# A drain behind each GpSimd mask, clamp and cast in an attention and ELU feed-forward kernel

## The chip, the core and the metric

The kernel runs on one core of a Trainium2 chip. The metric is device time in microseconds: how long one execution takes on the chip. A core has five engines that run their own instruction streams side by side and wait for each other through semaphores: TensorE (PE, matmuls), VectorE (DVE), ScalarE (ACT), GpSimd (POOL) and SyncE (SP, which issues most transfers here). Transfers run on 16 DMA engines that all issuers share.

## What is computed

Attention with a causal mask over 576 positions, in front of which stand 16 "beacon" keys and values that every position may see; then a feed-forward layer with an ELU on the attention's output. 8 batches, 8 heads of 64, model width 512, inner width 2048.

```python
k_all = np.concatenate([beacon_k, k], axis=2)          # 16 + 576 keys
v_all = np.concatenate([beacon_v, v], axis=2)
scores = scale * np.matmul(q, k_all.transpose(0, 1, 3, 2))
causal[:, Nb:] = np.triu(np.ones((S, S), dtype=bool), k=1)
scores = np.where(causal, -1000000000.0, scores)
a = np.exp(scores - scores.max(-1, keepdims=True))
a /= a.sum(-1, keepdims=True) + 1e-09
out = np.matmul(a, v_all)                              # then (B * S, H * D)
h = x @ w_in
g = np.where(h > 0.0, h, np.exp(np.minimum(h, 0.0)) - 1.0)
return g @ w_out
```

## The kernel before

All work is written down first as a list of small operations (`Op`, lines 118 to 122), each with its engine or a choice of engines, the operations that it depends on, and the buffers that it takes and gives back. `Program.run` (lines 133 to 165) then goes through the table `ORDER`, made by hand, and emits the operations one by one. `PICKS` settles the engine where there is a choice (the letters P, V, A, G, S stand for TensorE, VectorE, ScalarE, GpSimd and SyncE), and `PLACES` settles the buffer. Nothing is moved afterwards: each engine runs its instructions in this order. The semaphores between engines are put in by the framework.

**Attention**, per batch and pair of heads. Loads of q, k and v go out on SP's queue (in the first batch on ACT's too) into float32 staging buffers (`st`, `vst`). A cast to 16 bits follows (`copy`, called from line 349 for a cast or a copy on DVE or POOL and from line 347 on ACT), into `sb` for q and k and into `v16` for v. For batches 0 to 3 PE transposes q and k (lines 393 to 453) and DVE and ACT copy them out of PSUM; from batch 4 on DMA transposes do it (line 508). Scores are matmuls with keys along the partitions (L542); the exponential is ACT's (L552), into a buffer `et`. The mask is POOL's (L557): an affine select that sets to zero what lies behind the diagonal, in place, in `et`. Then PE multiplies probabilities and values (L571), with a column of ones in v that gives the row sums, and DVE divides (L584, L585). The result is transposed by PE (L600) in batches 0 and 1 and by DMA (L591) from batch 2 on, into `xT`, a ring of three batches.

**Feed-forward**, in tiles of tokens: 128, 128 and 256 at first, then 512 each. A step is one bank of 512 columns: PE multiplies `xT` and `w_in` (L623), ACT takes the exponential (L630), the clamp brings that to at most 1 and at least 0, in place, in a buffer `wide` (L638 on POOL or DVE, in another form on ACT at L636), and DVE joins it with the matmul's own result, which gives ELU (L649). The second matmul with `w_out` is plain in the three small tiles (L760); the tiles of 512 tokens use a scheme of seven products in place of eight (L705), for which DVE forms sums and differences (L678 to L687, L722). Results go out from `wide`.

**Weights.** `w_in` and `w_out` come in four parts each, eight loads in all, which POOL issues (`load_w`, line 528, issue at L533). They are float32 in memory and are made float16 on the way. In POOL's order they stand between masks, clamps and casts of the first batches and small tiles: four parts of `w_in` first, then four of `w_out`.

POOL thus has five kinds of work: 142 masks, 72 clamps, 59 casts, 8 weight loads, and a few fills at the start. A mask is waited for by PE (L571), a clamp by DVE (L649), a cast of q and k by PE (L442 and others) or by SP (L508), and a cast of v by PE. SP also waits for casts, since a staging buffer can be loaded again only after its cast. In the first 25 us PE also runs 80 matmuls on a tile of ones, written into banks that nobody uses at that time (L352, the negative entries in `ORDER`).

The functions that the change touches, and what calls them:

Of the kernel before, what the change touches and what calls it, by code (L numbers as in the profile page):

```python
# [124 lines left out]
class Program:  # L125
# [7 lines left out]
    def run(self, order, picks, places, fill):  # L133

        picks, places, used = iter(picks), iter(places), set()
        for op in self.ops:  # L140
            if len(op.engines) > 1:
                op.eng = next(picks)
                assert op.eng in op.engines
        for i in order:
            if i < 0:
                at = int(next(places), 36)
                assert ("bank", at) not in used
                fill(self.rooms["bank"][at])
                continue
            op = self.ops[i]  # L150
            assert not op.done and all(d.done for d in op.deps)
            got = []
            for room in op.take:
                at = int(next(places), 36)
                assert (room, at) not in used
                used.add((room, at))
                op.held.append((room, at))
                got.append(self.rooms[room][at])
            if op.fn is not None:
                op.fn(self.engines[op.eng], *got, *op.args)  # L160
            for other, i in op.give:
                used.remove(other.held[i])
            op.done = True
        kept = {room for op in self.ops if op.keep for room in op.held}
        assert all(op.done for op in self.ops) and used == kept and next(places, None) is None
# [927 lines left out]
```

## Time and profile before

| | us |
|---|---|
| three runs | 335.48, 337.19, 337.56 (median 337.19) |
| the profiled execution | 334.36 |
| its span, from the first to the last instruction | 332.6 |
| PE busy | 324.6 |
| ACT, DVE, POOL busy | 244.4, 254.0, 160.2 |
| POOL: masks (L557), clamps (L638), casts into `sb` from `st` (L349) | 63.4, 45.1, 29.5 |
| longest sum of waits on POOL: clamps for ACT (L630), masks for ACT (L552) | 62.5, 54.1 |

How to read the lines in the next part: a row of the timeline has the start and the length in us, the engine, the line of the kernel, the operation, the tiles written and read, the shape, a count, and in brackets how long the engine had been idle before and what ended that. A row with a count above 1 stands for instructions that follow each other. In a table of stages the columns are the stretch, its length, the busy time with the number of instructions, the clock that TensorE was granted, the mean share of the DMA engines at work and the GB/s moved. A row of a source line has the count of the instructions, then their durations in ns (least, median, most) and the first and last start. An engine's name with a q behind it is its sequencer, which issues transfers and runs drains and semaphore instructions; those are not counted as busy.

### The profile page before, as it was taken

What the parts mean: (1) busy time and instruction counts of PE and PEld (TensorE: products, weight loads), DVE (VectorE), ACT (ScalarE), POOL (GpSimd) and SP (SyncE); (2) the same over time, 40 slices, a digit from 0 to 9 for tenths busy, and PEclk for the clock granted to TensorE, in tenths of its full rate; (3) what the DMA queues carried; (4) which work ended last, traced back from release to release, by engine and by line L of the source; (5) the groups of instructions that cost most, each with busy time, mean ns of one, the idle gap of its engine ahead of it and who ended that gap; (6) DMA issues with size and microseconds to landing.
All of it is one profiled execution on the core that took longest, in us unless ns stands there. A gap on an engine that the chain in (4) does not pass through costs nothing.

```text
span 332.6 us, 9782 instructions
## 1 busy us (share of the span) xinstructions
PE 324.6 (98%) x3784; PEld 233.9 (70%) x3784; DVE 254.0 (76%) x587; ACT 244.4 (73%) x475; POOL 160.2 (48%) x289
## 2 busy tenths in 40 slices
PE   8999999999999999999999999999999999999995
PEld 6678877545678558878847787557877895456884
DVE  4687786689997499667869984699639973889862
ACT  2797799887986985789989957887678835766410
POOL 3596995376767472474544531645165500214100
PEclk9999999999999999999999999999999999999999
DMA  7999999899866878595599956996480065000015
GB/s 214 248 246 229 218 271 239 246 314 200 159 181 113 163 173 197 114 169 109 106 190 205 159 120 184 197 155 134 110 153 34 33 143 169 0 3 32 21 55 179
DMA packets 131902, 51.43 MB, mean 155 GB/s; under 512 B 113424, under 2 KB 128272, under 8 KB 131856
## 3 DMA queue, kind: packets, MB, share of 16 engines
q1 hardware_dynamic: 122160, 41.47, 59.8%
q0 software_dynamic: 4224, 4.19, 7.6%
q10 hardware_dynamic: 5472, 5.15, 5.3%
q8 instruction: 29, 0.48, 0.6%
q14 instruction: 17, 0.14, 0.1%
HBM read 37.22 MB, written 9.44 MB: 140 GB/s over the span
## 4 chain that ended last, share of the span: by engine, by line
PE 84%; DMA 5%; POOL 3%; DVE 3%; issue 2%; ACT 1%; SPq 0%; POOLq 0%; DVEq 0%
PE bank L623 36%; PE bank L705 28%; PE bank L571 8%; PE bank L542 6%; PE bank L760 4%; DMA w_in<-in_moe_w_in_dram 3%; POOL et L557 2%; PE bank L442 1%; DMA st<-in_k_dram 1%; DMA st<-in_q_dram 1%; DVE gt L684 1%; DVE gt L649 1%; POOL sb L349 1%; DVE ss L678 0%; POOL w_in L533 0%
## 5 line engine op out<-in xcount | busy, mean ns | idle before, releaser
L623 PE MATMUL bank<-xT,w_in 128*128 128x512 f16 (+5 forms) x832 | 132.9, 314 | 0.4 <-DMA w_in<-in_moe_w_in_dram 0.3
L552 ACT ACTIVATE et<-bank 128x512 f16<-128x512 f32 (+3 forms) x220 | 108.5, 588 | 20.8 <-PE bank L542 18.0
L649 DVE SCALAR_TENSOR_TENSOR gt<-wide,bank 128x512 f16<-128x512 f32 x144 | 94.2, 688 | 23.1 <-POOL wide L638 14.1
L623 PEld LDWEIGHTS <-w_in 128*128 128x128 f16 x832 | 71.0, 98 | 48.7 <-issue 1.1
L630 ACT ACTIVATE wide<-bank 128x512 f32<-128x512 f32 x144 | 83.0, 600 | 25.1 <-PE bank L623 22.5
L557 POOL TENSOR_SCALAR_AFFINE_SELECT et<-et 128x256 f16<-128x256 f16 (+3 forms) x142 | 63.4, 467 | 55.2 <-ACT et L552 54.1
L705 PEld LDWEIGHTS <-gt 128*128 128x128 f16 x768 | 72.6, 98 | 13.8 <-issue 1.7
L638 POOL TENSOR_SCALAR wide<-wide 128x512 f32<-128x512 f32 x72 | 45.1, 633 | 70.8 <-ACT wide L630 62.5
L705 PE MATMUL bank<-w_out,gt 128*128 128x256 f16 x512 | 63.2, 273 | 0.0
L349 POOL CAST sb<-st 128x1024 bf16<-128x1024 f32 (+6 forms) x32 | 29.5, 931 | 21.9 <-DMA st<-in_q_dram 13.0
L571 PE MATMUL bank<-v,et 128*128 128x65 f16 (+1 forms) x960 | 37.9, 193 | 0.5 <-issue 0.5
L571 PEld LDWEIGHTS <-et 128*128 128x128 f16 (+1 forms) x960 | 35.4, 97 | 4.1 <-issue 1.2
L585 DVE TENSOR_TENSOR x<-bank,rl 128x256 f16<-128x256 f32 (+2 forms) x68 | 32.1, 472 | 2.4
L347 ACT ACTIVATE wide<-bank 128x512 f32<-128x512 f32 x24 | 14.4, 608 | 25.9 <-PE bank L705 23.8
L542 PE MATMUL bank<-qT,kT 64*128 64x80 bf16 (+4 forms) x752 | 32.9, 224 | 0.1
L705 PE MATMUL bank<-wt,gt 128*128 128x256 f16 x256 | 31.6, 273 | 0.9 <-DVE gt L684 0.5
L542 PEld LDWEIGHTS <-kT 64*128 64x128 bf16 x752 | 20.8, 95 | 12.0 <-issue 8.8
L638 DVE TENSOR_SCALAR wide<-wide 128x512 f32<-128x512 f32 x34 | 16.2, 477 | 10.8 <-ACT wide L630 10.7
L636 ACT ACTIVATE wide<-wide 128x512 f32<-128x512 f32 x38 | 23.9, 631 | 0.8
L722 DVE TENSOR_TENSOR wide<-bank,wide 128x512 f32<-128x512 f32 x24 | 16.3, 686 | 9.1 <-PE bank L705 6.4
L349 DVE COPY kT<-bank 128x16 bf16<-128x16 bf16 (+4 forms) x48 | 16.2, 448 | 6.4 <-PE bank L450 2.5
L584 DVE RECIPROCAL rl<-bank 128x4 f32<-128x4 f32 (+2 forms) x68 | 12.3, 181 | 10.8 <-PE bank L571 8.0
(64 smaller groups left out, 249.2 us busy)
## 6 DMA issues: line engine op xcount, KB each, us to landing
vst<-in_v_dram SPq DMA_DIRECT2D x23, 256.0 KB, 4.5
out_dram<-wide SPq DMA_DIRECT2D x18, 256.0 KB, 2.6
out_dram<-wide ACTq DMA_DIRECT2D x17, 256.0 KB, 2.7
st<-in_q_dram SPq DMA_DIRECT2D x16, 256.0 KB, 4.8
st<-in_k_dram SPq DMA_DIRECT2D x12, 256.0 KB, 4.2
w_in<-in_moe_w_in_dram POOLq DMA_DIRECT2D x4, 512.0 KB, 9.9
w_out<-in_moe_w_out_dram POOLq DMA_DIRECT2D x4, 512.0 KB, 9.9
st<-in_k_dram SPq DMA_DIRECT2D x7, 288.0 KB, 6.7
```

The costliest lines, as they stand in the source:

```text
L349: e.tensor_copy(out=out, in_=in_)
L542: e.matmul(out=banks[h][:, o:o + w], lhsT=kT[D * h:D * h + D, P * jc:P * jc + P], rhs=qT[D * h:D * h + D, q0:q0 + w], start=True, stop=Tru ...
L552: e.activation(out=et[:, h, 0:w], in_=scs[n, u][h][:, 0:w], func=AFT.Exp, bias=0.0, scale=float(1.0 / (D ** 0.5)))
L557: e.affine_select(out=part, in_=part, compare_op=ALU.is_ge, fill=fill0, base=q0 + NB - P * jc, pattern=[[0, 2], [0, times], [1, dw]], chan ...
L571: e.matmul(out=av[:, c:c + D + 1], lhsT=ets[tuple(unit)][0:m, h, col:col + P], rhs=v16s[b % 2][0:m, jc, 2 * hp + h, 0:D + 1], start=(jc == ...
L585: e.tensor_tensor(out=x16s[b % 2][:, blks[0]:blks[-1] + 1:step, P * hp:P * hp + P].rearrange("q i (h d) -> q i h d", d=D), in0=av[:, :, :, ...
L623: e.matmul(out=bank[:, o:o + z - a], lhsT=w_in16[:, cc, P * fc:P * fc + P], rhs=xTa[:, cc, a % RING:a % RING + z - a], start=(cc == 0), st ...
L630: e.activation(out=t, in_=hpss[p, i], func=AFT.Exp, bias=0.0, scale=1.0)
L636: e.activation(out=t, in_=t, func=AFT.Relu, bias=1.0, scale=-1.0)
L638: e.tensor_scalar(out=t, in0=t, scalar1=1.0, scalar2=0.0, op0=ALU.min, op1=ALU.max)
L649: e.scalar_tensor_tensor(out=out, in0=in0, scalar=-1.0 if (p, i) in below else 1.0, in1=in1, op0=ALU.mult if (p, i) in below else ALU.subt ...
L705: e.matmul(out=bank[:, HC * s:HC * s + HC], lhsT=left[:, c, P * s:P * s + P], rhs=RIGHT[k][:, fc], start=(fc == 0 and s == 0 and k in HEAD ...
```

## The change

Behind each operation that `Program.run` emits on GpSimd, except for the weight loads, a drain is emitted on GpSimd. A drain is an instruction without operands: the engine goes on to its next instruction when what it has under way is finished.

```diff
             if op.fn is not None:
                 op.fn(self.engines[op.eng], *got, *op.args)
+                if op.eng == "G" and op.fn.__name__ != "load_w":
+                    self.engines["G"].drain()
             for other, i in op.give:
                 used.remove(other.held[i])
             op.done = True
```

In the built program these are 273 drains on POOL, one behind each mask, clamp and cast. None of them waits for a semaphore or raises one. All other instructions stand on their engines in the order that they had, with the same buffers. The masks, clamps and casts raise the semaphores that they raised before. Only which of eight semaphores some of the transfers on SP's and ACT's queues raise is shifted, and with it the names in the waits for those transfers. The line numbers behind line 160 are two higher in the changed kernel: L557 becomes L559, and so on.

## Prediction

> **What bounds the kernel now.** I read the page of the profile first: busy shares, then the chain that ended last.
>
> ```profile
> PE 324.6 (98%) x3784; PEld 233.9 (70%) x3784; DVE 254.0 (76%) x587; ACT 244.4 (73%) x475; POOL 160.2 (48%) x289
> ...
> PE 84%; DMA 5%; POOL 3%; DVE 3%; issue 2%; ACT 1%; SPq 0%; POOLq 0%; DVEq 0%
> ```
>
> PE is busy 98% of the 332.6 us span and carries 84% of the chain. POOL is at work for 48%, so the average says that it has time to spare. But PE has none: what POOL delivers late, after PE's instruction in line has been reached, is lost for good, since PE's order is fixed. So the question is where POOL has no idle time. The table of POOL's busy time by stage answers it; its columns are the stretch, its length, then busy time and instructions.
>
> ```profile
> 13.30:17.66 4.36, 4.35 (x10) 1.00 1.08 263
> 17.66:49.79 32.13, 28.57 (x51) 1.00 1.15 239
> 49.79:56.98 7.19, 4.93 (x11) 1.00 1.17 241
> ```
>
> ```profile
> 60.00:80.00 20.00, 12.65 (x20) 1.00 1.10 279
> 80.00:100.00 20.00, 12.94 (x21) 1.00 0.79 173
> 100.00:120.00 20.00, 12.54 (x24) 1.00 0.77 153
> 120.00:150.00 30.00, 16.18 (x31) 1.00 0.79 155
> ```
>
> From 13.30 to 49.79 POOL is nearly full (32.9 of 36.5 us); behind 60 it works some 63% of the time or less. The head is therefore the place. POOL's timeline there (start, length, line, count, and in brackets the idle time ahead):
>
> ```profile
> 13.31 0.42 POOL L557 TENSOR_SCALAR_AFFINE_SELECT et<-et 128x256 f16<-128x256 f16 x1 [2.42 <-ACT et L552]
> ...
> 14.35 1.53 POOL L557 TENSOR_SCALAR_AFFINE_SELECT et<-et 128x256 f16<-128x256 f16 x4
> ...
> 17.67 0.90 POOL L533 DMA_DIRECT2D w_in<-in_moe_w_in_dram  x1
> 18.59 0.63 POOL L557 TENSOR_SCALAR_AFFINE_SELECT et<-et 128x160 f16<-128x160 f16 x1
> ...
> 29.50 0.62 POOL L638 TENSOR_SCALAR wide<-wide 128x512 f32<-128x512 f32 x1 [1.90 <-ACT wide L630]
> ...
> 32.55 0.60 POOL L638 TENSOR_SCALAR wide<-wide 128x512 f32<-128x512 f32 x1 [0.62 <-ACT wide L630]
> ...
> 34.79 0.61 POOL L638 TENSOR_SCALAR wide<-wide 128x512 f32<-128x512 f32 x1 [0.47 <-ACT wide L630]
> ...
> 38.57 0.61 POOL L638 TENSOR_SCALAR wide<-wide 128x512 f32<-128x512 f32 x1 [0.26 <-ACT wide L630]
> ...
> 48.99 0.79 POOL L533 DMA_DIRECT2D w_out<-in_moe_w_out_dram  x1
> 49.80 1.65 POOL L557 TENSOR_SCALAR_AFFINE_SELECT et<-et 128x160 f16<-128x160 f16 x4
> ```
>
> Two things are to be seen. All eight weight loads are issued by POOL in this stretch, the first at 17.67, the last at 48.99, mixed with masks, clamps and casts. And the waits that could take up a delay are few: 1.90 + 0.62 + 0.47 + 0.26, with some smaller ones about 3.4 us up to 49.80.
>
> **The change, part by part.** It removes and moves nothing. It adds 273 drains, one behind each of 142 masks, 72 clamps and 59 casts. A drain signals nobody; a mask's consumer is released by the mask itself as before. What is queued behind a drain is POOL's next instruction. Where that one would have waited anyway the drain costs nothing: the wait covers it.
>
> *A drain as such.* The trace has no drain between two working instructions, so its price is bounded by the nearest rows.
>
> ```profile
> 0.80 0.20 POOL masks.py:197 MEMSET identb<- 128x128 bf16 x1 [0.29 <-POOLq L1077]
> 1.08 0.29 POOL masks.py:199 TENSOR_SCALAR_AFFINE_SELECT identb<-identb 128x128 bf16<-128x128 bf16 x1
> ```
>
> This select has to wait for the end of the memset ahead of it and starts 0.08 us behind that end. Without such a wait four masks take 1.53 us (14.35, above), 0.37 to 0.38 apart though each lasts 0.42: they overlap by 0.04. So the loss of overlap costs at least 0.12 us. On top comes the drain itself. The closing and opening drains:
>
> ```profile
> L1088 POOLq DRAIN  x3: 40/93/1407, 312.3 to 332.4; - x3
> ...
> L1088 DVEq DRAIN  x2: 19/374/730, 326.9 to 332.2; - x2
> L1088 ACTq DRAIN  x2: 8/80/152, 329.7 to 332.1; - x2
> ```
>
> ```profile
> L1077 POOLq DRAIN  x1: 183/183/183, 0.4 to 0.4; - x1
> ```
>
> Two of POOL's closing drains, with nothing left to wait for, last 0.04 and 0.09 us; the sum is 0.16 to 0.21 and I take 0.17, near the low end, since part of it hides behind the 0.08. The high end is the third closing drain of 1407 ns, which began at 312.3; the last clamp ended at 312.96:
>
> ```profile
> 312.35 0.61 POOL L638 TENSOR_SCALAR wide<-wide 128x512 f32<-128x512 f32 x1 [0.39 <-ACT wide L630]
> ...
> 326.90 0.69 DVE L722 TENSOR_TENSOR wide<-bank,wide 128x512 f32<-128x512 f32 x1 [0.98 <-PE bank L705]
> ```
>
> It went on for 0.75 us past that end, where DVE's closing drain (326.9 + 0.73) ended 0.04 us past its last instruction. So 0.12 to 0.87 us for a drain.
>
> *A drain behind a weight load.* That odd 0.75 us is the clue on which the forecast rests. It is the only drain in the trace with POOL's eight loads ahead of it; the two drains that follow it are short again, and so is the opening one with no load ahead (0.18 us, past four memsets). I read it as POOL settling the books of its loads, about 0.09 us for each of the eight, all landed long before. If a drain settles loads, one that comes while a load is under way must stay until the load lands. POOL writes the transfer itself (the load counts as 0.8 us of POOL's work, where SP and ACT only issue), so nobody else could say when it is finished. Against it speaks ACT's closing drain: begun at 329.7 and over in 0.15 us, while a store that ACT had issued at 329.33 needed 2.1 us to land.
>
> ```profile
> 329.33 0.35 ACTq L732 DMA_DIRECT2D out_dram<-vst  x1
> ...
> out_dram<-vst ACTq DMA_DIRECT2D x1, 128.0 KB, 2.1
> ```
>
> But that transfer goes by another queue, which ACT's program does not write. The price of this reading: landing times of the loads from the two ends of the stretch, and over all eight.
>
> ```profile
> w_in<-in_moe_w_in_dram POOLq DMA_DIRECT2D x1, 512.0 KB, 9.9
> ...
> w_out<-in_moe_w_out_dram POOLq DMA_DIRECT2D x1, 512.0 KB, 9.5
> ...
> DMA to landing us min/median/max: 8.5/9.9/12.0
> ```
>
> Issued at 17.67 and 48.99, the first and last land at 27.6 and 58.5: one load each (58.5 - 27.6)/7 = 4.4 us, since they queue behind each other. Behind drains they no longer queue; a load alone takes between 0.8 (issue) + 4.4 = 5.2 and 9.9 us. The first meets the same traffic as now and keeps 9.9; for the other seven I take the middle, 7.6, because the other queues' bytes are spread over twice the time. From each landing time go the issue and the one instruction that runs beside the transfer, together 1.5 us (0.63 us behind the first load, 1.2 where a cast follows). Stalls: 9.9 + 7 x 7.6 - 8 x 1.5 = 51 us; with 5.2 for all 30, with 9.9 for all 67.
>
> *The sum.* Up to 17.67 ten instructions, 10 x 0.17 = 1.7. From there to 49.80 the table has 51, of which 8 loads and one that reaches in from the left: 42 x 0.17 = 7.1. Less the 3.4 us of waits. POOL is late at 49.80 by 1.7 + 51 + 7.1 - 3.4 = 56.4 us. Who waits for that: matmuls of values with probabilities (L571), and behind them all of PE.
>
> ```profile
> 54.84 2.15 POOL L557 TENSOR_SCALAR_AFFINE_SELECT et<-et 128x160 f16<-128x160 f16 x6 [1.90 <-ACT et L552]
> ```
>
> ```profile
> 56.73 0.43 PE L571 MATMUL bank<-v,et 128*128 128x65 f16 x9
> ```
>
> These masks end at 56.99 and L571 starts within 0.3 us of them: no slack. Eleven drains more (1.9) against two waits (2.25) leave 56 us for PE. The last load is issued after seven of the stalls, at 48.99 + 50 = 99, and lands near 107, 48 us later than now: less than the masks behind it, and covered by them. Behind 60 POOL's 12.5 us of work in 20 grow by 20 to 24 x 0.17, about 4; it fits, with here and there a mask just late: 1.5 us. The traced execution took 334.4 us (span 332.6), so 334.4 + 56 + 1.5 = 392. It is 2.8 below the median of the runs shown, which I add: 395. With stalls of 30 and 67 the same sum gives 374 and 411.
>
> A page speaks against this. The Trainium skill, Perfetto Trace Analysis, section "DMA Instruction — SWDGE (GPSIMD)", lets a load issued by GpSimd end, for the engine, once its cores have written the last descriptor; the data move later. By that rule a drain would be through 0.8 us after the issue, no stall would be left, and the sum would be that of rival A. The first load's row (0.90 us, the next mask at 18.59) agrees with it for the mask that follows; no row shows it for a drain.
>
> **The rivals.**
> - A: a drain waits for instructions alone. The head then gives 1.7 + 7.1 - 3.4 = 5.4 at 49.80, and 5 on PE; with 1.5 behind it 334.4 + 6.5 + 2.8 = 344, and 337 to 347 for 0.12 to 0.21 us a drain and some slack. For it: ACT's drain. Against it: the 0.75 us.
> - C: every drain costs like the closing one, 0.87 us. POOL becomes the bound: 160.2 + 273 x 0.87 = 398 us, and the 20 us from its last clamp to the end: near 420. Against it: the short drains of the same engine.
> - D, not slower: drains overlap with what they follow, and the head's own waits take them up. 52 drains against 3.4 us of waits: the point is 0.065 us a drain. Below it nothing arrives late and the time stays at 337. Against it: the select that starts 0.08 us behind the end it waits for, 0.12 in all.
>
> **How the numbers follow.** My forecast 0.80, A 0.11, C 0.05, D 0.04. The range 371 to 420 holds nearly all of the first (374 to 411, and a little for a PE that resumes slowly) and half of C: about 8 in 10. A measurement here tells about 1% from no change, 340.6 us: D and half of A lie within it, 0.09; faster 0.01; slower 0.90.
>
> **What would show it.** In the profile after, POOL's first two instructions behind each of the eight loads should lie 5 to 9 us apart, where they now follow at once, with no other engine named as the cause; landing times of the loads near 7.6 and no queue among them; the last load issued near 99 instead of 48.99; PE idle some 50 us before 115 and hardly after. If masks behind a load follow it within a microsecond, the step on loads is wrong and A holds. If plain masks lie 0.8 us or more apart where they are now 0.38, C holds. If their distance is still below 0.45, D does. The forecast is also wrong if loads alone land in under 5 us.

## The result, and the profile after

| | before | after |
|---|---|---|
| four runs each, median us | 337.24 (335.48 to 337.56) | 391.18 (388.29 to 391.65) |
| the profiled execution, us | 334.36 | 388.29 |
| its span, us | 332.6 | 386.6 |
| ratio after / before | | 1.159, interval 1.153 to 1.166 |

The changed kernel is 54 us slower; the forecast was 395, within 371 to 420. The page after, busy shares and the chain that ended last:

```profile
PE 342.3 (89%) x3784; PEld 244.7 (63%) x3784; DVE 258.2 (67%) x587; ACT 245.9 (64%) x475; POOL 165.4 (43%) x289
...
PE 38%; issue 23%; POOLq 22%; DMA 5%; DVE 4%; ACT 3%; SPq 2%; POOL 2%; ACTq 0%; DVEq 0%
```

The engines have the same instructions in the same numbers. PE's share of the chain fell from 84% to 38%, and 45% of it are now "issue" and "POOLq": POOL's sequencer, and time for which the profile names no cause. POOL itself is at work for a smaller share than before (43%, from 48%). Who reads busy shares alone would call POOL the engine with the most room.

POOL's timeline shows where the time lies (columns as in the prediction). The first and second load, and the last:

```profile
14.54 2.08 POOL L559 TENSOR_SCALAR_AFFINE_SELECT et<-et 128x256 f16<-128x256 f16 x4
...
19.70 0.90 POOL L535 DMA_DIRECT2D w_in<-in_moe_w_in_dram  x1 [0.65 <-issue]
20.63 0.53 POOL L559 TENSOR_SCALAR_AFFINE_SELECT et<-et 128x160 f16<-128x160 f16 x1
29.75 0.61 POOL L351 CAST v<-vst 128x512 f16<-128x512 f32 x1 [8.59 <-issue]
...
33.72 0.77 POOL L535 DMA_DIRECT2D w_in<-in_moe_w_in_dram  x1 [0.59 <-issue]
34.50 0.43 POOL L559 TENSOR_SCALAR_AFFINE_SELECT et<-et 128x256 f16<-128x256 f16 x1
39.30 0.88 POOL L559 TENSOR_SCALAR_AFFINE_SELECT et<-et 128x224 f16<-128x224 f16 x2 [4.37 <-issue]
...
91.08 0.79 POOL L535 DMA_DIRECT2D w_out<-in_moe_w_out_dram  x1 [0.56 <-issue]
91.89 0.40 POOL L559 TENSOR_SCALAR_AFFINE_SELECT et<-et 128x160 f16<-128x160 f16 x1
98.67 1.50 POOL L559 TENSOR_SCALAR_AFFINE_SELECT et<-et 128x256 f16<-128x256 f16 x3 [6.39 <-issue]
```

Each load is followed by one instruction, which starts at once, and then by a hole: 8.59, 4.37, 3.60, 4.80, 4.06, 4.00, 4.32 and 6.39 us, 40.1 in all. For the first two and the last two the profile names nothing. For the four between them it names ACT, as in this row behind the third load:

```profile
49.28 0.61 POOL L640 TENSOR_SCALAR wide<-wide 128x512 f32<-128x512 f32 x1 [3.60 <-ACT et L554]
```

There the next instruction had to wait for ACT as well, but ACT's release came 0.1 to 0.8 us before the drain's end, so the drain ended last in these four too. The four masks at 14.54, with no load ahead of them, lie farther apart than they did (2.08 us for the four, 1.53 before), but only by some 0.18 us each. The lines of the drains, of the closing drain and of the loads (durations in ns; landing in us):

```profile
L162 POOLq DRAIN  x273: 182/682/9947, 2.9 to 366.3; - x137
```

```profile
L1090 POOLq DRAIN  x3: 34/41/88, 367.0 to 386.3; - x3
```

```profile
DMA to landing us min/median/max: 5.3/5.7/9.9
```

The longest drain, 9.947 us, is the one behind the first load. It ends at 29.66 and the load lands at 29.57. All eight drains of this kind end 0.08 to 0.09 us after the landing of the load ahead of them. And the closing drain, 1407 ns before, is now 88 ns at most: there is nothing left for it to settle.

What became of the delay downstream is read from PE. The waits on POOL that PE now has, in total us, times, and the longest:

```profile
PE bank L573 <- POOL et L559: 14.8, 9, 5.8
PE bank L573 <- POOL v L351: 10.5, 3, 9.5
```

The table by stage (columns as in the prediction, for PE, PEld, DVE, ACT and POOL in turn, then clock, DMA share and GB/s):

```profile
20.00:40.00 20.00, 7.14 (x111) 5.33 (x108) 4.96 (x18) 5.64 (x14) 5.52 (x12) 0.64 0.92 197
40.00:60.00 20.00, 15.40 (x197) 13.35 (x198) 9.05 (x28) 11.16 (x24) 9.17 (x14) 0.84 0.52 109
60.00:80.00 20.00, 13.23 (x113) 11.33 (x113) 7.55 (x13) 6.54 (x13) 8.30 (x13) 0.59 0.47 82
80.00:100.00 20.00, 10.29 (x111) 5.97 (x110) 7.45 (x17) 6.95 (x15) 7.89 (x17) 0.76 0.71 162
100.00:120.00 20.00, 20.00 (x218) 11.82 (x216) 11.81 (x29) 15.53 (x30) 9.05 (x17) 0.90 0.45 120
```

Between 20 and 100 PE is idle for 33.9 us, and what it does there goes at a granted clock of 0.59 to 0.84. From 100 to 120 it has no idle time. To see how late PE is, one matches pieces of the chain that are the same work: before,

```profile
88.41 1.91 PE bank L705 x16
...
276.53 18.99 PE bank L623 x88
```

and after,

```profile
138.20 1.91 PE bank L707 x16
...
330.45 18.99 PE bank L625 x88
```

PE is 49.8 us late at the first pair and 53.9 at the second. Matched in the same way it is 49.4 late in the work that began at 55 before, so nearly the whole loss is made in the head and some 4.5 us come later.

### The profile page after: what moved, and what is told of

Same layout as the page of the kernel before. It is cut to its first block, busy times and chain, and to the rows that moved or that the text cites. A ratio compares the mean times of both kernels' runs of the same rounds, so it can differ in the third digit from the quotient of the medians.

```text
span 386.6 us, 10055 instructions
## 1 busy us (share of the span) xinstructions
PE 342.3 (89%) x3784; PEld 244.7 (63%) x3784; DVE 258.2 (67%) x587; ACT 245.9 (64%) x475; POOL 165.4 (43%) x289
## 3 DMA queue, kind: packets, MB, share of 16 engines
q0 software_dynamic: 4224, 4.19, 7.1%
## 4 chain that ended last, share of the span: by engine, by line
PE 38%; issue 23%; POOLq 22%; DMA 5%; DVE 4%; ACT 3%; SPq 2%; POOL 2%; ACTq 0%; DVEq 0%
POOLq L162 22%; PE bank L707 15%; PE bank L625 13%; PE bank L573 4%; PE bank L544 3%; DMA st<-in_q_dram 2%; PE bank L762 2%; DMA st<-in_k_dram 2%; DVE gt L651 2%; ACT et L554 2%; DVE wide L640 1%; SPq L510 1%; POOL w_in L535 1%; ACT wide L632 1%; PE bank L444 1%
## 5 line engine op out<-in xcount | busy, mean ns | idle before, releaser
L625 PE MATMUL bank<-xT,w_in 128*128 128x512 f16 (+5 forms) x832 | 138.3, 324 | 5.7 <-DVE gt L651 5.2
L625 PEld LDWEIGHTS <-w_in 128*128 128x128 f16 x832 | 75.9, 103 | 54.9 <-issue 7.6
L559 POOL TENSOR_SCALAR_AFFINE_SELECT et<-et 128x256 f16<-128x256 f16 (+3 forms) x142 | 63.4, 446 | 82.7 <-ACT et L554 51.1
L573 PE MATMUL bank<-v,et 128*128 128x65 f16 (+1 forms) x960 | 42.1, 199 | 25.4 <-POOL et L559 14.8
L573 PEld LDWEIGHTS <-et 128*128 128x128 f16 (+1 forms) x960 | 38.3, 101 | 31.1 <-POOL et L559 16.7
L544 PE MATMUL bank<-qT,kT 64*128 64x80 bf16 (+4 forms) x752 | 35.8, 232 | 6.1 <-DVE gt L651 5.1
L544 PEld LDWEIGHTS <-kT 64*128 64x128 bf16 x752 | 22.1, 98 | 20.2 <-issue 16.9
L640 DVE TENSOR_SCALAR wide<-wide 128x512 f32<-128x512 f32 x34 | 17.7, 521 | 10.2 <-ACT wide L632 10.1
```

Source lines behind the costliest of these rows:

```text
L544: e.matmul(out=banks[h][:, o:o + w], lhsT=kT[D * h:D * h + D, P * jc:P * jc + P], rhs=qT[D * h:D * h + D, q0:q0 + w], start=True, stop=Tru ...
L559: e.affine_select(out=part, in_=part, compare_op=ALU.is_ge, fill=fill0, base=q0 + NB - P * jc, pattern=[[0, 2], [0, times], [1, dw]], chan ...
L573: e.matmul(out=av[:, c:c + D + 1], lhsT=ets[tuple(unit)][0:m, h, col:col + P], rhs=v16s[b % 2][0:m, jc, 2 * hp + h, 0:D + 1], start=(jc == ...
L625: e.matmul(out=bank[:, o:o + z - a], lhsT=w_in16[:, cc, P * fc:P * fc + P], rhs=xTa[:, cc, a % RING:a % RING + z - a], start=(cc == 0), st ...
L640: e.tensor_scalar(out=t, in0=t, scalar1=1.0, scalar2=0.0, op0=ALU.min, op1=ALU.max)
```

## The experiments

The load theory says that a GpSimd drain stays until the loads that GpSimd issued ahead of it have landed. Its rivals are that the sum of many small drains makes the loss, and that what slows the kernel is something beside the wait (the lower clock, or the drains' nearness to the loads). All edits stand in `Program.run`, behind the line that emits an operation, and start from the kernel before, unless it is said otherwise; counters and flags are set to zero, False or None ahead of the loop. Medians are in us, and each ratio is against runs of the kernel before that were taken beside it.

### Eight drains, behind the loads alone

```diff
+                if op.eng == "G" and op.fn.__name__ == "load_w":
+                    under_way = True
+                elif op.eng == "G" and under_way:
+                    self.engines["G"].drain()
+                    under_way = False
```

> Eight drains alone, each behind the first instruction that follows a weight load; the other 265 are left out. Load theory (a GpSimd drain stays until the load that GpSimd issued has landed): the changed kernel's landings were 9.9 us for the first, 5.3 to 5.8 for the next six and 7.5 for the last, some 51 us in all; less 8 x 1.5 that runs beside them and 3.4 of waits that take up the delay, 36 us, so 337 + 36 = 373, between 368 and 380. Rival (the drains' own price does it, 0.2 us each, in the stretch where POOL is full): 8 x 0.2 = 1.6, so 337 to 340.

Measured: 379.7, ratio 1.128 (1.120 to 1.137). POOL's timeline at the first load and up to the second:

```profile
18.07 0.90 POOL L539 DMA_DIRECT2D w_in<-in_moe_w_in_dram  x1
18.99 0.58 POOL L563 TENSOR_SCALAR_AFFINE_SELECT et<-et 128x160 f16<-128x160 f16 x1
28.25 0.61 POOL L355 CAST v<-vst 128x512 f16<-128x512 f32 x1 [8.68 <-issue]
28.80 1.85 POOL L563 TENSOR_SCALAR_AFFINE_SELECT et<-et 128x160 f16<-128x160 f16 x5
30.61 0.77 POOL L539 DMA_DIRECT2D w_in<-in_moe_w_in_dram  x1
```

Eight of the 273 drains make 43 of the 54 us. The hole behind the first load is the one of the changed kernel (8.68, there 8.59), and nothing is spaced out elsewhere. The point of 373 was too low: it took the landing times of the changed kernel, some 51 us in all, and here they sum to 56.6. The run without the drains ahead of the loads, below, bears on that.

### The other drains: late ones, then those of the head

Drains from the twelfth operation behind the last load on, 205 of them, with no load under way:

```diff
+                if op.eng == "G":
+                    loads += op.fn.__name__ == "load_w"
+                    since += loads == 8
+                    if since > 12:
+                        self.engines["G"].drain()
```

> Drains behind the masks, clamps and casts from the twelfth behind the last weight load on, when all loads have landed: some 200 of the 273, none ahead of that. Load theory: only the plain price where POOL has idle time, 3 to 5 us: 340 to 342. Rival (the drains' own price): three quarters of the drains bring a large share of the 54 us, 355 or more.

Measured: 340.73, ratio 1.014 (1.007 to 1.020). PE's new waits are small and few (total us, times, longest):

```profile
PEld L577 <- POOL et L563: 3.4, 5, 1.0
PE bank L577 <- POOL et L563: 2.5, 4, 0.9
```

So 205 drains cost some 4.5 us altogether (0.0135 of 337): masks that come up to 1 us late, as the forecast had it, but more of them.

The other part, 68 drains up to that place:

```diff
-                    if since > 12:
+                    if since <= 12 and op.fn.__name__ != "load_w":
                         self.engines["G"].drain()
```

> Drains behind the masks, clamps and casts up to the twelfth behind the last weight load, 68 of the 273; none after that. If the parts add up, the changed kernel less what the 205 later drains cost alone (a ratio of 1.0135): 1.1594 - 0.0135 = 1.146, 386 us, and some 6 us more than the eight drains behind the loads alone (1.1283). If the plain drains of the head are covered by the stalls (POOL would only wait there for the landing): the same as those eight alone, 380. If the later drains cost more once PE has fallen behind: below 384.

Measured: 386.17, ratio 1.147 (1.142 to 1.152). Against the eight drains alone that is 0.019, some 6 us (give or take 3), for 60 plain drains in the head. The two parts add up: 0.147 for the head and 0.014 for the late drains make 1.161, where the whole has 1.159, and 1.156 where it ran beside the head's drains.

### No drain: a semaphore wait for the load

At the place of each of the eight drains POOL copies one element per partition of the weights just loaded into a small tile of its own. The copy reads what the load writes, so it waits for the landing by a semaphore.

```diff
+                if op.fn.__name__ == "load_w":
+                    under_way = op.args
+                elif op.eng == "G" and under_way:
+                    self.touch(*under_way)
+                    under_way = None
...
+    seen = konst.tile([P, 16], FP16, name="seen")
+
+    def touch(which, f4):
+        src = w_in16[:, 0, 512 * f4:512 * f4 + 1] if which == 0 else w_out16[:, 4 * f4, 0:1]
+        nc.gpsimd.tensor_copy(out=seen[:, 8 * which + f4:8 * which + f4 + 1], in_=src)
+
+    plan.touch = touch
```

> No drain at all. At the same eight places POOL copies one element of the part of the weights that was just loaded, so that it must wait for the landing by semaphore. Load theory: the same stalls as with eight drains, within 4 us of that kernel: 368 to 380. Rival (a drain does something of its own beyond waiting for the landing, in the queue or with the clock): clearly less than with eight drains, under 360.

Measured: 378.98, ratio 1.127 (1.117 to 1.136). The timeline at the first load:

```profile
17.51 0.90 POOL L539 DMA_DIRECT2D w_in<-in_moe_w_in_dram  x1
18.43 0.57 POOL L563 TENSOR_SCALAR_AFFINE_SELECT et<-et 128x160 f16<-128x160 f16 x1
27.64 0.19 POOL L1074 COPY seen<-w_in 128x1 f16<-128x1 f16 x1 [8.63 <-DMA w_in<-in_moe_w_in_dram]
```

The same hole, 8.63 us, now has its cause beside it: the DMA of `w_in`. A wait for the landing, said openly, costs what the drain costs (1.127 against 1.128). All eight holes name the DMA of their load here, and they sum to 45.8 us, as they do with the eight drains (45.9). This is the plainest evidence for the load theory: the hole that the profile calls "issue" is a wait for a transfer.

### One drain, behind the fifth load

```diff
+                if op.eng == "G":
+                    loads += op.fn.__name__ == "load_w"
+                    if loads == 5 and op.fn.__name__ != "load_w":
+                        self.engines["G"].drain()
+                        loads = 9
```

> One drain alone, behind the first instruction that follows the fifth weight load. Load theory: one stall. That load is queued behind the fourth there, so that its landing time is near the 8.5 to 9.9 us of the kernel before: a stall of 8.5 to 9.9 less 1.5, less waits of POOL behind it of 0.3: 6 to 8 us on POOL; PE takes most of it, 4 to 8 us: 341 to 345. Rival (the drains' own price): 0.2 us, 337.

Measured: 344.87, ratio 1.023 (1.019 to 1.027). The drain, and the place on POOL's timeline:

```profile
L165 POOLq DRAIN  x1: 9201/9201/9201, 35.3 to 35.3; - x1
```

```profile
35.38 0.78 POOL L539 DMA_DIRECT2D w_out<-in_moe_w_out_dram  x1
36.20 0.62 POOL L644 TENSOR_SCALAR wide<-wide 128x512 f32<-128x512 f32 x1
44.58 0.61 POOL L644 TENSOR_SCALAR wide<-wide 128x512 f32<-128x512 f32 x1 [7.76 <-issue]
```

A single instruction without operands costs 2.3%. PE is 7.8 us late from 45 on, the length of the hole, and 9.0 at the end: none of it is won back.

### Drains on ScalarE, behind its own transfers

22 drains on ACT, each behind a load or store that ACT issues, and none on GpSimd.

```diff
+                if op.eng == "A" and op.fn.__name__ in ("load_k", "load_k2", "load_k3", "load_q", "load_q3", "load_v", "do_store", "do_put", "do_put2"):
+                    self.engines["A"].drain()
```

> A drain on ACT behind each of the transfers that ACT issues (stores of the output, a few loads at the start); none on GpSimd. If a drain waits only for transfers that the engine itself writes, as GpSimd does with the weight loads: no wait for the landing, 336 to 339. Rival (a drain waits for any transfer that its engine has issued): over 20 transfers of 2 to 3 us each on an engine that is busy 73%, 10 to 50 us more, 347 or more.

Measured: 336.61, ratio 1.003 (0.999 to 1.007). The drains' durations, and the landing of most of the transfers ahead of them:

```profile
L162 ACTq DRAIN  x22: 163/370/2043, 1.4 to 333.3; - x22
```

```profile
out_dram<-wide ACTq DMA_DIRECT2D x17, 256.0 KB, 2.5
```

A store takes 2.5 us to land, and the median drain is over in 0.37. All 22 drains end at least 1.0 us before the transfer ahead of them has landed, the longest one (2.04) too. So a drain on this engine does not wait for the transfers that the engine issued. The wait for landings belongs to GpSimd's drain behind GpSimd's loads. Whether the engine or the queue makes the difference stays open: the page of the profile has the 4.19 MB of GpSimd's loads on a queue of the kind software_dynamic and all other data on hardware_dynamic queues, and no run has an engine issue on the other's kind.

### No drain directly ahead of a load

In the changed kernel POOL is idle for 0.55 to 0.65 us ahead of each load, behind the drain that stands there. I took these 8 x 0.58 = 4.6 us for a price of that drain. This kernel is the changed one less those eight drains.

```diff
+        mine = [self.ops[i] for i in order if i >= 0 and self.ops[i].eng == "G" and self.ops[i].fn]
+        ahead = {id(x) for x, y in zip(mine, mine[1:]) if y.fn.__name__ == "load_w"}
...
+                if op.eng == "G" and op.fn.__name__ != "load_w" and id(op) not in ahead:
+                    self.engines["G"].drain()
```

> The changed kernel without the eight drains that stand directly ahead of a weight load. In the changed kernel POOL was idle for 0.55 to 0.65 us between such a drain and the load, where a mask follows its drain after 0.1 to 0.2. If the load's preparation is what a drain ahead of it lays bare: 8 x 0.6 = 4.8 us less, 385 to 388. Rival (that idle time is the load's own and is there without a drain, or PE is not held up by it): 390 to 392.

Measured: 389.8, ratio 1.155 (1.151 to 1.160): as slow as the changed kernel. At the fourth load:

```profile
52.36 1.14 POOL L353 CAST sb<-st 128x1152 bf16<-128x1152 f32 x1 [0.24 <-issue]
53.44 0.79 POOL L537 DMA_DIRECT2D w_in<-in_moe_w_in_dram  x1
54.27 0.63 POOL L642 TENSOR_SCALAR wide<-wide 128x512 f32<-128x512 f32 x1
59.98 0.42 POOL L561 TENSOR_SCALAR_AFFINE_SELECT et<-et 128x256 f16<-128x256 f16 x1 [5.09 <-issue]
```

```profile
DMA to landing us min/median/max: 5.5/6.4/10.2
```

The idle time ahead of the load is gone; the load overlaps the cast by 0.06 us. (Ahead of the first three loads 0.02 to 0.13 us are left.) But the loads now land 0.7 us later after their start at the median (6.4 against 5.7; the eight together 55.5 against 50.8). The two kernels with a wait behind each load and no drain ahead of it agree: the landing times sum to 56.6 us with the eight drains and to 57.5 with the copies. I read what looked like idle time as some 0.55 us of preparation of the load, which shows as a gap when a drain keeps it from starting beside the instruction ahead, and as a longer landing otherwise; no row shows the preparation by itself. My expectation was wrong: without the drain the time is the same, so the term is no price of it.

### Two drains for each

The changed kernel with each drain doubled.

```diff
                 if op.eng == "G" and op.fn.__name__ != "load_w":
                     self.engines["G"].drain()
+                    self.engines["G"].drain()
```

> The changed kernel with two drains in place of each. The second finds POOL idle and costs its own time, 0.04 to 0.09 us, and one place in the sequencer: some 50 in the full stretch, 3 to 5 us, and 1 to 2 behind it: 394 to 399. If the price of a drain is only the overlap that is lost between instructions, the second adds nothing: 390 to 392.

Measured: 401.0, ratio 1.192 (1.186 to 1.197), above what I expected. POOL's timeline in the head:

```profile
14.55 0.42 POOL L560 TENSOR_SCALAR_AFFINE_SELECT et<-et 128x256 f16<-128x256 f16 x1 [0.21 <-issue]
15.17 0.42 POOL L560 TENSOR_SCALAR_AFFINE_SELECT et<-et 128x256 f16<-128x256 f16 x1 [0.20 <-issue]
...
24.86 0.90 POOL L536 DMA_DIRECT2D w_in<-in_moe_w_in_dram  x1 [5.34 <-issue]
```

Between plain instructions the distance from an end to the next start rises from 0.15 us at the median to 0.21: the second drain costs some 0.065 us. What was not expected is the 5.34 us ahead of the first load, where no load is under way. Half of it is given back, since the hole behind that load is 5.98 us here and 8.59 in the changed kernel. Around that time two packets go by on a queue of instructions:

```profile
q14 instruction: 2, 0.02, 0.9%
```

The first ran from 22.9 to 23.2 us, inside the gap, the second at 24.9, when the load had begun. That POOL waited for instructions is a guess: the gap goes on for 1.6 us past the end of the first packet, and what held POOL there is open. Of the 12.7 us by which the profiled execution is longer than that of the changed kernel, 5.8 lie in the head (PE is 55.1 us late behind it, not 49.4) and 6.9 behind it. Why the second drains cost more there than the 1 to 2 us that I expected, no run shows.

### The clock

PE's clock fell where it waited. To see whether that costs time, the changed kernel with 16 matmuls on the tile of ones ahead of each of the products of values and probabilities in the first two batches:

```diff
+        for _ in range(16 if b < SH else 0):
+            fill(av)
```

> The changed kernel with 16 matmuls on the tile of ones ahead of each product of probabilities and values in the first two batches, so that PE works while it waits; nothing reads what they write. The granted clock of the changed kernel lay between 0.59 and 0.90 in the stretches from 20 to 120 us. Clock theory (PE's half clock behind each stall holds up the chain): the clock rises to nearly 1 and the time falls by 3 us or more, below 388. Load theory (PE waits for POOL there, its clock is covered): within 2 us, 389 to 393, or longer if the fills themselves get in the way.

Measured: 399.36, ratio 1.185 (1.181 to 1.189). Two stretches of the table by stage:

```profile
40.00:60.00 20.00, 20.00 (x287) 17.77 (x285) 8.42 (x29) 8.95 (x22) 8.14 (x12) 1.00 0.36 90
60.00:80.00 20.00, 13.61 (x134) 12.09 (x132) 6.41 (x12) 8.55 (x17) 7.25 (x11) 0.74 0.51 74
```

The clock is higher (1.00 and 0.74, against 0.84 and 0.59), and the kernel is 8 us slower than the changed one, since the fills stand in the way when a mask does come. The run gives the clock no part in the loss, but it can't exclude a small one, because it pays for the clock with work. The better argument is POOL's own timeline in the changed kernel. From 20.63 to 98.67 it has no idle time but the holes behind the loads, the gaps ahead of them, and at most 0.24 us between two other instructions, so a slower PE did not hold it up. At the end of that stretch POOL is 48.6 us late, and PE is 49.4 us late soon behind it. That leaves 0.8 us for the clock there. PE waits for POOL anyway, and slower matmuls fill time that was lost.

### The changed kernel once more

> The changed kernel once more, on the same chip as the kernel with the head's drains alone, so that the two can be compared: 388 to 392.

Measured: 389.16, ratio 1.156 (1.151 to 1.161), as in the first result.

## Why the prediction was right

The mechanism held, and the total came out 4 us below the forecast. Two of its terms were off, in opposite directions. By its own steps:

- *A drain as such*, 0.17 us. Before, an instruction started 0.04 us ahead of its predecessor's end; after, 0.15 us behind it at the median. That is 0.19. The reading of the bounds (0.12 from the overlap, and a little of the short closing drains) was good.
- *A drain behind a load waits for the landing*: right. Eight drains that end 0.08 us behind the landing show it, eight drains alone that cost 12.8%, and an explicit wait for the same landing that costs 12.7%. The clue was the right one, too, and other traces bear it out. The closing drains of the kernel that waits by copies, of the one with a drain behind the fifth load, and of the one with eight drains:

```profile
L1101 POOLq DRAIN  x3: 40/93/1407, 358.2 to 378.3; - x3
L1094 POOLq DRAIN  x3: 46/93/984, 321.3 to 341.3; - x3
L1094 POOLq DRAIN  x3: 40/89/731, 358.8 to 379.0; - x3
```

With eight loads since the last drain the longest ends 0.75 us past the last clamp, even though a semaphore had told POOL of each landing; with three loads, 0.33; with none, 0.08. In the kernel with the late drains alone the first of them, 0.2 us behind the last landing, takes this over (0.75 us past its cast). So the first drain behind loads that have landed pays some 0.085 us for each of them (the prediction had 0.09), and a wait by semaphore does not take that away. What POOL does in this time no run shows. One reason that I gave does not hold: that nobody but POOL could say when a load is finished. The copies waited for it by a semaphore. ACT's short drain was rightly set aside as evidence: 22 more of them behave like it, on their own engine alone.
- *The stalls*, 51 us. This term was too large. A load alone lands in 5.3 to 6.1 us in six of the eight cases, near my low end of 5.2, not in the 7.6 that I took from the middle; only the first (9.9) and the last (7.4) take longer. The holes sum to 40.1. I should have taken the low end: 4.4 us was the distance of landings under full traffic, and in the holes the traffic itself falls (82 GB/s from 60 to 80, where it was 239 in the stretch of the loads before).
- *The preparation of a load*, about 0.55 us for each of the eight, I did not foresee. It returns 4.6 us of the 11. The run without the drains ahead of the loads shows that it is no price of theirs: without them the time is the same and the landings are longer.
- *POOL's lateness*, 56.4 at 49.80. Measured 48.6: 2.0 up to the first load, 40.1 of holes, 4.0 ahead of the other seven loads, some 5 us of plain drains, less the 3.4 of waits, make 47.7; 0.9 are left without a row.
- *Behind the head*, 1.5 us. It was 4.5. The late drains alone give as much. POOL's work there fits in the time, as the forecast said, but masks come late by up to 1 us at more places than I counted, for each mask waits out its own predecessor's drain.
- *The sum*: 334.4 + 49.4 on PE in the head + 4.5 behind it = 388.3, and the profiled execution took 388.29. The forecast had 334.4 + 56 + 1.5 = 392. Of the 3.6 us between them, the head was 6.6 too long (its stalls, less what the preparation gives back) and the later part 3.0 too short, so the closeness owes something to errors that cancel.

The Trainium skill's rule that I set against my reading (Perfetto Trace Analysis, section "DMA Instruction — SWDGE (GPSIMD)": the end that the profile gives such a load is when the last descriptor is written, not when the data have moved) holds for the instruction behind the load: the mask at 20.63 starts 0.03 us behind the issue that began at 19.70. It does not tell what a drain does; there the trace has 8.59 us where the rule would give none, and the measurement decides.

The rivals: A (a drain waits for instructions alone, 344) describes the drains that have no load under way, and the runs price these at 0.019 + 0.014 of 337, some 11 us, where A had 6.5. For the eight behind the loads it is refuted by the hole behind each of them. C (0.87 us for every drain) falls with the four masks that need 2.08 us in place of 1.53. D (drains for nothing) falls with the same row: 0.18 us a drain is above its point of 0.065. What a second drain adds is 0.065 us.

Of the marks that I named: the first two instructions behind a load start 4.7 to 9.1 us apart, as foreseen, but only four of the eight times with no engine named, since ACT is named at the other four; the last load is issued at 91.08, not 99, by the shorter stalls; landing times are near 5.7, not 7.6; PE's loss before 100 is 33.9 us of idle time, and the rest of its 49 is the same matmuls at a lower clock (67.6 us of work up to that point, where it was 51.9), which I had not foreseen.

Left open: whether the weight loads, issued by another engine, would take the price of the drains away; that was not tried on the chip. No version here beats the kernel before.

## What to carry to other kernels

In these runs a drain on GpSimd was also a wait for the loads that GpSimd itself had issued and that had not landed; before you put one in for order or for safety, look at what its engine has under way, and let a semaphore of the one instruction that matters do the work. When an engine's share of busy time says that it has room, look for the stretch in which it has none: here one drain in that stretch cost 2.3%, and 205 outside of it 1.4%. And when the profile names no cause for a hole ("issue"), put an explicit wait for the suspect in its place: if the time stays the same, you have its name.

## What the hardware showed that was not expected

- GpSimd's drain ends 0.08 to 0.09 us after the landing of the load, eight times of eight; a drain right behind another costs some 0.065 us.
- The first GpSimd drain behind loads that landed before still takes some 0.085 us for each of them (0.75 us past the last instruction for eight, 0.33 for three, 0.08 for none).
- A load of 512 KB alone lands in 5.3 us at the least, some 0.55 us ahead of its recorded start, which I read as its preparation, not counted. Eight that queue behind each other took 9.9 each at the median, but one every 4.4 us, so waiting for each costs far more than it speeds each up.
- PE's granted clock fell to a mean of 0.59 in a stretch in which it had 13.2 us of work in 20.
- Once a GpSimd sequencer with more instructions stood still for 5.3 us ahead of a load; a packet of instructions was fetched in that time, but the cause is open.
